# The transfer queue of a fused convolution and expert kernel: issue order by the program instead of by the scheduler

## The chip, the cores and the metric

The program runs on one core of a Trainium2 chip. The metric is the device time of one execution in microseconds. Before the change the median of three runs is 1215.89 us (1215.02 to 1219.19). The profile was taken on a fourth execution.

## The reference, cut to what matters

```python
def _attn_ref(x, weight_gen):                 # x: 8 x 3584 x 192, weight_gen: 8 x 3584 x 8 x 7
    w = np.exp(weight_gen - np.max(weight_gen, axis=-1, keepdims=True))
    w = w / (np.sum(w, axis=-1, keepdims=True) + 1e-09)
    x_pad = np.concatenate([np.zeros((B, 6, D)), x], axis=1)
    x_unf = x_pad[:, idx, :].reshape(B, S, 7, 8, 24)
    return np.einsum('bshk,bskhg->bshg', w, x_unf).reshape(B, S, D)

def _moe_ref(x, w_gate, w1, w2):              # x: 28672 x 192; 8 experts, 192 -> 1024 -> 192
    logits = x @ w_gate
    expert_idx = np.argmax(logits, axis=1)
    gate_w = softmax(logits)[arange(N), expert_idx]
    ...
    h = np.maximum(x_sorted[lo:hi] @ w1[e], 0.0)      # tokens lo:hi are those of expert e
    y_sorted[lo:hi] = h @ w2[e]
    ...
    return gate_w[:, None] * y
```

A convolution over seven tokens, whose weights differ from token to token, is followed by a layer of experts of which each token uses one.

## The kernel before, in words

**Chunks.** The 28672 tokens are cut into 28 chunks of 1024. For each chunk `load` (L304, L314) brings `w_sb` and `x_sb`; VectorE multiplies and adds the taps (L355, L379), in the first four chunks with help of TensorE (L364) and GpSimd. The sum is split into a high and a low fp16 part (`pl`), TensorE transposes it (L474) and computes the gate's logits (L486), VectorE finds expert, rank and gate factor, and `send` (GpSimd, L560) scatters the token rows into the DRAM tensor `queue`, which holds a list of rows for each expert.

**Tiles.** After each chunk `choose` picks expert tiles that can be filled from the rows written so far: 256 tokens each at first, then 384, then small ones that empty the lists, 97 in all. The number of a tile's first row is computed on VectorE and lies in a small tile `rows` (L600). `fetch(n)` brings tile n in with four steps on SyncE (SP): it loads the row number into a register (`value_load`, L732; a TENSOR_LOAD in the order), it transposes the token rows into `xt` (L744), it loads the 1796 KB of the expert's weights into `wt` (L746), and it loads the gate factors and the output rows into `meta` (L749). `xt` waits until the scatters of the chunk that the tile was chosen from have landed and until the first layer has freed the buffer three tiles before; `wt` waits for the second layer of the tile three before; `meta` waits for the output scatters of the tile four before. The program calls `fetch` of tile n+2 in the middle of tile n. For the tiles of the last chunk seven more buffers are used, so that `fetch` may run up to nine tiles ahead.

**Layers.** TensorE computes the first layer (L806) and second layer (`l2`, L712) of neighbouring tiles in alternation, ScalarE and VectorE make `hh` and `hl` (L815 to L829), and GpSimd scatters the results to the output (L560).

**Two stages.** In the first `with` block (L954 to L967) the experts' weights are loaded, normalized, split into high and low halves and stored to `wq` in DRAM (L286 to L291), beside the convolution of the first chunks. In the second (L968) the tiles run beside the convolution of the other chunks. In both, the order on each engine is made by a scheduler that simulates times, except for VectorE in the second stage: `manual_schedule` keeps that one in the program's order. SP's order is the scheduler's own, so that a step of `fetch` may stand ahead of, or behind, steps that the program wrote earlier. SP issues strictly in its order: a step that waits holds up all that stands behind it.

**Rows at the end.** `pad_queues` (called after the last chunk's `send`) writes 128 zero rows behind each expert's list by eight scatters on GpSimd, and writes the 512 dummy rows that a spare tile reads, by four transfers of SP (L635) from `padrow`, which is filled at the program's start. The scheduler placed these four in the first stage.

Of the kernel before, what the change touches and what calls it, by code (L numbers as in the profile page):

```python
# [114 lines left out]
def conv_moe_kernel(ctx: ExitStack, tc: tile.TileContext, x, wgen, w_gate, w1, w2, out):  # L115
# [135 lines left out]
    def w_norm(e):  # L251


        g = ps_y.tile([P, 2, 2 * P], F32, name="y")
        for n, f in enumerate(wsp[e]):
            v = f.bitcast(BF16)
            if n:
                v = v.rearrange("p f d -> p (f d)")
            v = v.rearrange("p (b q t) -> p b q t", q=P, t=2)
            for b in range(12):  # L260
                blk = v[:, b, :, 1]
                nc.tensor.matmul(g[:, n, 0:P], blk, blk, start=(b == 0), stop=(b == 11))
        nc.vector.tensor_reduce(stats[e], g[:, :, 0:P], axis=AX.X, op=ALU.max)

    def w_high(e, pro):
        f1, f2 = wsp[e]
        ws, h1, l1, w2v = w_views(e)
        st2 = ps_y.tile([P, 2 * 256], F32, name="y")
        nc.tensor.matmul(st2[:, 0:2], ones_f, stats[e], start=True, stop=True)
        s, i = norm_scale(st2[:, 0:2], 2, pro)  # L270
        nc.vector.tensor_tensor(ws[:, W_INV:W_INV + 2].bitcast(F32), i[:, 0:1], i[:, 1:2], op=ALU.mult)
        nc.scalar.activation(h1, f1, AF.Copy, scale=s[:, 0:1])
        nc.scalar.activation(w2v[:, :, 0, :], f2, AF.Copy, scale=s[:, 1:2])
        wsp[e].append(s)

    def w_low(e):
        f1, f2, s = wsp[e]
        ws, h1, l1, w2v = w_views(e)
        nc.vector.scalar_tensor_tensor(l1, f1, s[:, 0:1], h1, **sub)
        yield  # L280
        nc.vector.scalar_tensor_tensor(w2v[:, :, 1, :], f2, s[:, 1:2], w2v[:, :, 0, :], **sub)
        yield
        r0 = e * P
        hl = ws[:, 0:3 * F].rearrange("p (t c) -> p t c", t=2)
        tails = wq[:, O_H1:].rearrange("q (t c) -> q t c", t=2)
        nc.sync.dma_start(wq[r0:r0 + P, 0:2 * F].rearrange("p (t c) -> p t c", t=2), hl[:, :, 0:F])  # L286
        nc.sync.dma_start(wq[r0:r0 + P, O_W2:O_H1], ws[:, 3 * F:])
        for i in range(2):
            half = hl[64 * i:64 * i + 64, :, F:]
            for r in (r0, r0 + 64):  # L290
                nc.sync.dma_start(tails[r:r + 64, :, i * FH:(i + 1) * FH], half)  # L291
# [8 lines left out]
    def load(c):  # L300
        k = ch[c] = Chunk()
        k.x = cin.tile([P, J + HALO, D], F32, name="x_sb")
        k.w = cin.tile([P, J * H, KW], F32, name="w_sb")
        nc.sync.dma_start(k.w, bass.AP(wr.tensor, wr.offset + c * J * H * KW,  # L304
                                       [[NP * H * KW, P], [1, J * H * KW]]))
        if c == 0:
            nc.vector.memset(k.x[0:1, 0:HALO, :], 0.0)
            for p0, p1 in ((1, PPB), (PPB, P)):
                nc.sync.dma_start(k.x[p0:p1, 0:HALO, :],
                                  bass.AP(xr.tensor, xr.offset + (p0 * NP - HALO) * D,  # L310
                                          [[NP * D, p1 - p0], [1, HALO * D]]))
            nc.sync.dma_start(k.x[:, HALO:, :], bass.AP(xr.tensor, xr.offset, [[NP * D, P], [1, J * D]]))
        else:
            nc.sync.dma_start(k.x, bass.AP(xr.tensor, xr.offset + (c * J - HALO) * D, [[NP * D, P], [1, (J + HALO) * D]]))  # L314
# [241 lines left out]
    def scatter(dst, idx, src, grp, bound=None):  # L556
        kw = {}
        if bound is not None:
            kw = dict(bounds_check=bound, oob_is_err=False)
        st = nc.gpsimd.indirect_dma_start(out=dst, out_offset=bass.IndirectOffsetOnAxis(ap=idx, axis=0),  # L560
                                          in_=src, in_offset=None, **kw)
        tc.declare_no_dep(st.ins, group=grp, reason="every row is written once")
        if grp == "q":
            tc.declare_no_dep(st.ins, group="qr", reason="a row is read only after it was written")
        tc.add_to_no_dep_group(grp, st.ins)
        return st
# [58 lines left out]
    def pad_queues():  # L625
        padi = const.tile([P, E], I32, name="padi")
        pio = const.tile([P, 1], F32, name="pio")
        nc.gpsimd.iota(pio, pattern=[[0, 1]], base=0, channel_multiplier=1,
                       allow_small_or_imprecise_dtypes=True)
        nc.vector.tensor_scalar(padi, base[-1], pio, None, op0=ALU.add)  # L630
        for e in range(E):
            st = scatter(queue, padi[:, e:e + 1], padrow, "q")
            writers[NCH - 1].append(st.ins.name)
        for n in range(4):
            st = nc.sync.dma_start(queue[DUMMY + n * P:DUMMY + (n + 1) * P, :], padrow)  # L635
            tc.declare_no_dep(st.ins, group="q", reason="every row is written once")
            tc.declare_no_dep(st.ins, group="qr", reason="a row is read only after it was written")
            tc.add_to_no_dep_group("q", st.ins)
            writers[NCH - 1].append(st.ins.name)
# [8 lines left out]
    def finish(c):  # L648

        yield max(0.0, ch[c].sent + REST1 - clock[0])  # L650
        logits(c)
        yield from route1(c)
        ranks(c)
        yield from gate(c)
        yield from places(c)
        send(c)
        if c == NCH - 1:
            pad_queues()
        yield from choose(c)
# [209 lines left out]
    def weights(pro):  # L869

        ev = []
        for e in range(E):
            at = W_AT + W_GAP * e
            ev += [(at, e, 0), (at + W_HIGH, e, 1), (at + W_LOW, e, 2)]
        for at, e, k in sorted(ev):
            yield at
            if k == 0:
                with tc.high_priority():
                    w_norm(e)
            elif k == 1:  # L880
                with tc.high_priority():
                    w_high(e, pro)
                clock[0] += 0.6
            else:
                low_ = w_low(e)
                while True:
                    with tc.high_priority():
                        if next(low_, 0) == 0:
                            break
                    clock[0] += 1.3  # L890
                    yield at
                if e + len(stage) < E:
                    with tc.high_priority():
                        w_load(e + len(stage), pro)
# [59 lines left out]
    with tc.tile_pool(name="pro", bufs=PROB) as pro, tc.tile_pool(name="pro1", bufs=1) as pro1:  # L954
        stats = [pro1.tile([P, 2], F32, name=f"st{e}") for e in range(E)]
        stage = [pro1.tile([P, W_STAGE], F16, name=f"ws{i}") for i in range(PROB)]
        for t in stage:
            nc.gpsimd.memset(t[:, W_INV:W_INV + 16], 0.0)
        load(0)
        for e in range(len(stage)):  # L960
            w_load(e, pro)
            if e == 0:
                load(1)
        wstream[0] = weights(pro)
        clock[0] = 5.0
        while wstream[0] is not None:
            vector_step()  # L967
    with tc.manual_schedule(engines={mybir.EngineType.DVE}):  # L968
        ffw = ctx.enter_context(tc.tile_pool(name="ffw", bufs=3, reuse_waits="tile"))
        ffx = ctx.enter_context(tc.tile_pool(name="ffx", bufs=2, reuse_waits="tile"))  # L970
        ffh = ctx.enter_context(tc.tile_pool(name="ffh", bufs=2, reuse_waits="tile"))
        ffo = ctx.enter_context(tc.tile_pool(name="ffo", bufs=6, reuse_waits="tile"))
        clock[1] = clock[0] + START
        parts = experts()
        n, _ = next(parts)
        while n is not None or parts is not None:
            if n is not None:
                while len(todo) <= n and vector_step():
                    pass
                if len(todo) <= n:  # L980
                    try:
                        parts.send(False)
                    except StopIteration:
                        break
                clock[1] = max(clock[1], todo[n][4] + FETCH)
            while clock[1] > clock[0] and vector_step():
                pass
            n, _ = parts.send(True)
# [23 lines left out]
```

## Time and profile before

| | |
|---|---|
| median of three runs | 1215.89 us |
| the profiled execution | 1220.97 us |
| its span | 1219.2 us |
| TensorE busy | 1143.4 us (94%) |
| VectorE busy | 1029.0 us (84%) |
| ScalarE, GpSimd busy | 695.5 us, 649.1 us |
| mean DMA rate | 263 GB/s |

TensorE is the busiest engine; over the span it is idle for 76 us. A part of this lies ahead of the first expert tile, where VectorE is the busy one. The rest of the page has to be read by stretches, since the stage of weights (to about 130 us), the small tiles (to about 290 us), the 384-token tiles (to about 1000 us) and the emptying of the lists (from there on) have different limits.

### The profile page before, as it was taken

Reading aid. Unit: us, or ns where it says so; the run is one execution under the profiler, and the core shown is the slowest. Engines: PE = TensorE matmul, PEld = TensorE weight load, DVE = VectorE, ACT = ScalarE, POOL = GpSimd, SP = SyncE. Lnnn points to the kernel's source line nnn. Section 1 sums busy time; section 2 is a strip of 40 time slices with the busy share of each in tenths; the row PEclk is TensorE's granted clock in tenths of the full one; section 3 lists DMA queues with packets and bytes.
Section 4 is the critical chain, followed back from the end, with each engine's and each line's share of the span. In section 5 each row is a group of like instructions: output and inputs, shape, how many; then the busy total and the mean of one; then the engine's idle time right before and its main releaser. Section 6 shows DMA issues by size and latency. Waiting matters only on the chain.

```text
span 1219.2 us, 30182 instructions
## 1 busy us (share of the span) xinstructions
PE 1143.4 (94%) x11666; PEld 934.5 (77%) x11666; DVE 1029.0 (84%) x1841; ACT 695.5 (57%) x1467; POOL 649.1 (53%) x576
## 2 busy tenths in 40 slices
PE   5688299899999999999999999999999998999997
PEld 3455299887787878787878777887877886789996
DVE  7999999899999999999999999999999964232331
ACT  3547277677656666665666556666664653443442
POOL 6884737565545456655566554556555565213222
PEclk9899599999999999999999999999999998999999
DMA  9998799998798768878787877788677668999995
GB/s 267 380 331 292 248 290 298 261 287 294 249 272 238 231 213 270 268 240 226 212 270 252 249 241 231 231 263 244 226 197 236 191 198 239 344 363 328 336 312 213
DMA packets 185134, 320.94 MB, mean 263 GB/s; under 512 B 132752, under 2 KB 156434, under 8 KB 169118
## 3 DMA queue, kind: packets, MB, share of 16 engines
q1 hardware_dynamic: 162862, 273.68, 72.5%
q0 software_dynamic: 22128, 45.33, 11.2%
q8 instruction: 91, 1.49, 0.5%
q14 instruction: 53, 0.43, 0.1%
HBM read 236.17 MB, written 60.76 MB: 244 GB/s over the span
## 4 chain that ended last, share of the span: by engine, by line
PE 70%; DVE 11%; DMA 9%; issue 6%; POOL 2%; SPq 1%; ACT 1%; POOLq 0%; DVEq 0%; ACTq 0%
PE ph L806 33%; PE y L712 30%; DVE tv L355 3%; DMA wt<-wq 3%; PE ph L819 2%; PE ph L474 2%; DVE hl L829 2%; DVE acc L379 1%; DMA f<-in_moe_w_dram 1%; DMA xt<-queue 1%; DMA x_sb<-in_x_dram 1%; POOL out_dram L560 1%; PE ph L364 1%; PE pm L486 1%; DMA wq<-ws 1%
## 5 line engine op out<-in xcount | busy, mean ns | idle before, releaser
L806 PE MATMUL ph<-xt,wt 128*128 128x384 f16 (+6 forms) x3880 | 579.8, 293 | 27.5 <-DMA wt<-wq 21.1
L712 PE MATMUL y<-wt,hh 128*128 128x192 f16 (+2 forms) x3696 | 505.9, 247 | 0.0
L560 POOL DMA_INDIRECT out_dram<-o,meta x231 | 277.8, 1203 | 410.7 <-ACT o L716 366.0
L712 PE MATMUL y<-wt,hl 128*128 128x192 f16 (+2 forms) x1848 | 451.6, 247 | 0.0
L806 PEld LDWEIGHTS <-wt 128*128 128x128 f16 x3880 | 330.3, 98 | 147.1 <-DMA wt<-wq 22.2
L712 PEld LDWEIGHTS <-hh 128*128 128x128 f16 (+2 forms) x3696 | 337.2, 99 | 32.9 <-issue 0.6
L560 POOL DMA_INDIRECT queue<-pl,pos x224 | 273.3, 1220 | 112.6 <-issue 70.4
L829 DVE SCALAR_TENSOR_TENSOR hl<-ph,hh 128x384 f16<-128x384 f32 (+2 forms) x372 | 203.7, 561 | 142.5 <-ACT hh L826 136.1
L355 DVE TENSOR_TENSOR tv<-x_sb,wp 128x1536 f32<-128x1536 f32 (+1 forms) x172 | 287.3, 1675 | 4.4 <-PE ph L364 4.1
L826 ACT ACTIVATE hh<-ph 128x384 f16<-128x384 f32 (+2 forms) x372 | 184.6, 500 | 185.3 <-PE ph L806 173.7
L379 DVE TENSOR_TENSOR acc<-acc,tv 128x1536 f32<-128x1536 f32 x144 | 250.0, 1736 | 0.0
L712 PEld LDWEIGHTS <-hl 128*128 128x128 f16 (+2 forms) x1848 | 181.9, 99 | 15.2 <-issue 0.3
L815 ACT ACTIVATE hh<-ph 128x384 f16<-128x384 f32 (+1 forms) x204 | 105.0, 519 | 75.2 <-PE ph L806 71.6
L716 ACT ACTIVATE o<-y,fac 128x192 f32<-128x192 f32 (+2 forms) x231 | 91.9, 420 | 86.1 <-PE y L712 84.6
L821 ACT ACTIVATE hl<-ph 128x384 f16<-128x384 f32 (+1 forms) x204 | 104.3, 519 | 41.0 <-PE ph L819 40.5
L476 ACT ACTIVATE xg<-ph 128x1024 f16<-128x1024 f16 x84 | 82.8, 1024 | 30.7 <-PE ph L474 28.8
L364 PE MATMUL ph<-tv,identf 128*128 128x384 f32 x168 | 63.6, 518 | 11.0 <-DVE tv L355 8.5
L819 PE MATMUL ph<-hh,negi 128*128 128x384 f16 (+1 forms) x256 | 68.7, 304 | 0.0
L414 ACT ACTIVATE junk<-x_sb 128x768 bf16<-128x768 f32 (+2 forms) x56 | 48.1, 859 | 18.4 <-DVE ssq L423 8.9
L474 PE MATMUL ph<-idh,pl 128*128 128x128 f16 x672 | 53.4, 225 | 3.1 <-ACT pl L445 1.6
L364 PEld LDWEIGHTS ph<-tv,identf 128*128 128x128 f32 x168 | 31.3, 199 | 30.4 <-DVE tv L355 11.4
L449 ACT ACTIVATE pl<-acc 128x768 f16<-128x768 f32 (+1 forms) x52 | 40.0, 813 | 24.3 <-DVE acc L379 16.0
(121 smaller groups left out, 810.7 us busy)
## 6 DMA issues: line engine op xcount, KB each, us to landing
wt<-wq SPq DMA_DIRECT2D x97, 1796.0 KB
x_sb<-in_x_dram SPq DMA_DIRECT2D x27, 1344.0 KB
w_sb<-in_weight_gen_dram SPq DMA_DIRECT2D x28, 224.0 KB
wq<-ws SPq DMA_DIRECT2D x8, 772.0 KB
f<-in_moe_w_dram SPq DMA_DIRECT2D x8, 768.0 KB
f<-in_moe_w_dram SPq DMA_DIRECT2D x8, 512.0 KB
wq<-ws SPq DMA_DIRECT2D x8, 512.0 KB
wq<-ws SPq DMA_DIRECT2D x32, 128.0 KB
```

The source lines that it names most:

```text
L355: eng.tensor_tensor(out, xs, ws, op=ALU.mult)
L364: nc.tensor.matmul(ap[:, 0:m], identf, tf[:, 2 * i * D:2 * i * D + m], start=(n == 0), stop=(n == KW - 1))
L379: eng.tensor_tensor(ac, ac, t, op=ALU.add)
L560: st = nc.gpsimd.indirect_dma_start(out=dst, out_offset=bass.IndirectOffsetOnAxis(ap=idx, axis=0), in_=src, in_offset=None, **kw)
L712: nc.tensor.matmul(y, hx[:, f, sl], w2v[:, f, t, :], start=(f == 0 and k == 0), stop=(f == NF - 1 and k == 2))
L716: nc.scalar.activation(o[0:m, :], y, AF.Copy, scale=fac[0:m, s:s + 1])
L806: nc.tensor.matmul(ph[:, g], wt[:, wc + f * P:wc + (f + 1) * P], xt[:, xc, 0:T], start=(k == 0 and g == 0), stop=(k == 4), skip_group_chec ...
L815: nc.scalar.activation(hv, ph, AF.Relu, scale=SHRINK)
L819: nc.tensor.matmul(ph[:, g], negi, hv[:, g], start=False, stop=True, skip_group_check=True)
L821: nc.scalar.activation(lv, ph, AF.Relu)
L826: nc.scalar.activation(hv, ph, AF.Relu)
L829: nc.vector.scalar_tensor_tensor(lv, ph, 0.0, hv, op0=ALU.max, op1=ALU.subtract)
```

## The change: who orders SP in the second stage, and where the dummy rows are written

```diff
@@ pad_queues
             st = scatter(queue, padi[:, e:e + 1], padrow, "q")
             writers[NCH - 1].append(st.ins.name)
+
+    def pad_dummies():
         for n in range(4):
             st = nc.sync.dma_start(queue[DUMMY + n * P:DUMMY + (n + 1) * P, :], padrow)
@@ first stage
             w_load(e, pro)
             if e == 0:
                 load(1)
+        pad_dummies()
         wstream[0] = weights(pro)
@@ second stage
-    with tc.manual_schedule(engines={mybir.EngineType.DVE}):
+    with tc.manual_schedule(engines={mybir.EngineType.DVE, mybir.EngineType.SP}):
```

In the second stage SP issues in the order in which the program calls `load` and `fetch`. The four dummy writes are called in the first stage, as SP would otherwise issue them after the last chunk's `send`. Lines behind the new function move down by two or three (L744 becomes L746, L746 becomes L748, L749 becomes L751).

SP at the first tiles, before. `xt_1515`, `wt_1517` and `meta_1519` are tile 0's, `xt_1530`, `wt_1532` and `meta_1534` tile 1's; four row numbers of later tiles stand between the weights and the rows of tile 1:

```order
L744 DMA_TRANSPOSE xt_1515<-queue_84 128x3x256
L746 ISA
L746 DMA wt_1517<-wq_85 128x7184
L749 ISA
L749 DMA meta_1519<-queue_84 128x2x2
L746 ISA
L746 DMA wt_1532<-wq_85 128x7184
L732 TENSOR_LOAD rows_1484
```

After, from tile 0's weights (`wt_1521`) to tile 1's (`wt_1536`):

```order
L748 DMA wt_1521<-wq_85 128x7184
L751 ISA
L751 DMA meta_1523<-queue_84 128x2x2
L734 TENSOR_LOAD rows_1275
L734 ISA x2
L746 ISA
L746 DMA_TRANSPOSE xt_1534<-queue_84 128x3x256
L748 ISA
L748 DMA wt_1536<-wq_85 128x7184
```

Tile 1's weights stood ahead of tile 1's transpose, and now stand behind it.

SP at tiles 8 and 9 before, where `xt_2822` is of tile 9, `wt_2652` of tile 8, and `x_sb_2831` is a chunk of the convolution:

```order
L744 DMA_TRANSPOSE xt_2822<-queue_84 128x3x256
L314 DMA x_sb_2831<-in_x_dram 128x2688
L746 ISA
L746 DMA wt_2652<-wq_85 128x7184
L749 ISA
L749 DMA meta_2654<-queue_84 128x2x2
L304 DMA w_sb_3349<-in_weight_gen_dram 128x448
```

After, from behind tile 8's weights (`wt_2656` is the transfer before the first row) to the same chunk (`x_sb_2835`):

```order
L751 DMA meta_2658<-queue_84 128x2x2
L734 TENSOR_LOAD rows_2311
L734 ISA x2
L746 ISA
L746 DMA_TRANSPOSE xt_2826<-queue_84 128x3x256
L748 ISA
L748 DMA wt_2828<-wq_85 128x7184
L751 ISA
L751 DMA meta_2830<-queue_84 128x2x2
L304 DMA w_sb_2836<-in_weight_gen_dram 128x448
L314 DMA x_sb_2835<-in_x_dram 128x2688
```

The next tile's transpose and the chunk's `x_sb` stood ahead of a tile's weights; now each tile's weights follow its own transpose, and the chunk comes behind the weights of two tiles.

SP in the last chunk, before, at tile 67 (`wt_16270`): behind its weights come ten row numbers, and only then its rows, `xt_16268`:

```order
L732 TENSOR_LOAD rows_16298
L732 ISA x2
L746 ISA
L746 DMA wt_16270<-wq_85 128x7184
L732 TENSOR_LOAD rows_16375
L732 ISA x2
```

After, the same tile, with its transpose first:

```order
L734 TENSOR_LOAD rows_15919
L734 ISA x2
L746 ISA
L746 DMA_TRANSPOSE xt_16268<-queue_84 128x3x384
L748 ISA
L748 DMA wt_16270<-wq_85 128x7184
```

Tile 67's weights moved from ahead of its transpose to behind it. In both programs that transpose waits for the last of the eight scatters of `pad_queues`. Between the early tiles and the last chunk the SP order reads the same in both but for the row numbers, which come one for each tile instead of in blocks, and for `w_sb` ahead of `x_sb`. VectorE's order differs only in the first 270 or so of its rows, where the stage of weights hands over: the last expert's two low halves (L279, L281) come earlier.

## Rows read from the trace of the kernel before

**Rows 1.** The busy time of the engines over the span, and the sizes of two transfers, from the page:

```profile
PE 1143.4 (94%) x11666; PEld 934.5 (77%) x11666; DVE 1029.0 (84%) x1841; ACT 695.5 (57%) x1467; POOL 649.1 (53%) x576
wt<-wq SPq DMA_DIRECT2D x97, 1796.0 KB
x_sb<-in_x_dram SPq DMA_DIRECT2D x27, 1344.0 KB
```

**Rows 2.** Windows: length, then busy time of each engine (and instructions), the granted clock, the DMA share and GB/s, in five stretches of the run:

```profile
120.00:160.00 40.00, 17.82 (x178) 15.23 (x176) 36.27 (x69) 13.83 (x27) 28.12 (x22) 0.63 0.80 253
200.00:240.00 40.00, 36.52 (x402) 33.83 (x400) 36.10 (x56) 26.25 (x54) 24.22 (x19) 0.96 0.93 269
...
320.00:630.00 310.00, 309.97 (x3090) 247.18 (x3088) 303.33 (x536) 194.89 (x423) 175.26 (x146) 1.00 0.82 244
630.00:730.00 100.00, 98.04 (x957) 77.79 (x955) 99.97 (x180) 59.55 (x133) 57.97 (x45) 1.00 0.76 241
...
1160.00:1200.00 40.00, 40.00 (x666) 39.96 (x664) 12.89 (x20) 17.69 (x40) 9.74 (x11) 1.00 0.98 346
```

**Rows 3.** What TensorE waited for from 133 to 320 us and, below the line of dots, from 990 us to the end (us in total, times, longest):

```profile
PE ph L806 <- DMA wt<-wq: 18.6, 4, 12.4
...
PE ph L806 <- DMA xt<-queue: 4.4, 1, 4.4
```

**Rows 4.** The timeline of SP's queue at the start of the second stage (start, duration, what):

```profile
134.86 1.34 SPq L744 DMA_TRANSPOSE xt<-queue  x1
136.74 0.37 SPq L746 DMA_DIRECT2D wt<-wq  x1
...
137.97 0.33 SPq L746 DMA_DIRECT2D wt<-wq  x1
146.88 1.39 SPq L744 DMA_TRANSPOSE xt<-queue  x1
```

**Rows 5.** The timeline of TensorE there; the last bracket is the idle time before and what ended it. Between the two rows of the second layer (L712) stand ten more of its matmuls:

```profile
145.79 5.66 PE L806 MATMUL ph<-xt,wt 128*128 128x256 f16 x32 [12.45 <-DMA wt<-wq]
151.51 1.04 PE L806 MATMUL ph<-xt,wt 128*128 128x256 f16 x8
...
152.60 0.33 PE L712 MATMUL y<-wt,hh 128*128 128x192 f16 x2
...
154.06 0.33 PE L712 MATMUL y<-wt,hh 128*128 128x192 f16 x2
154.23 2.35 PE L806 MATMUL ph<-xt,wt 128*128 128x256 f16 x20
```

**Rows 6.** The timeline of GpSimd: the last of the eight scatters of chunk 1 and of chunk 2.

```profile
123.76 3.71 POOL L560 DMA_INDIRECT queue<-pl,pos  x1 [0.30 <-issue]
139.91 1.37 POOL L560 DMA_INDIRECT queue<-pl,pos  x1 [0.30 <-issue]
```

**Rows 7.** From the chain of work, the pieces between 200 and 285 us in which a tile's weights were under way, and a piece of the second layer (start, duration, what):

```profile
215.49 12.44 DMA wt<-wq
249.45 10.88 DMA wt<-wq
270.19 1.99 PE y L712 x24
272.30 9.45 DMA wt<-wq
```

**Rows 8.** SP's queue around the first two of these:

```profile
212.59 0.38 SPq L749 DMA_DIRECT2D meta<-queue  x1
213.36 1.21 SPq L744 DMA_TRANSPOSE xt<-queue  x1
214.67 0.53 SPq L314 DMA_DIRECT2D x_sb<-in_x_dram  x1
215.49 0.33 SPq L746 DMA_DIRECT2D wt<-wq  x1
...
243.70 0.34 SPq L314 DMA_DIRECT2D x_sb<-in_x_dram  x1
```

**Rows 9.** What TensorE waited for from 630 to 730 us:

```profile
PE ph L806 <- DVE hl L829: 1.9, 2, 1.7
```

**Rows 10.** SP's queue in the last chunk, and, below the dots, the end of the pad scatters in the chain of work:

```profile
1006.80 0.34 SPq L746 DMA_DIRECT2D wt<-wq  x1
1020.14 1.33 SPq L744 DMA_TRANSPOSE xt<-queue  x1
...
1017.73 2.39 DMA queue<-padrow,padi
```

**Rows 11.** TensorE's timeline around tile 67's first matmul:

```profile
1018.96 1.79 PE L806 MATMUL ph<-xt,wt 128*128 128x384 f16 x10
1025.13 1.76 PE L806 MATMUL ph<-xt,wt 128*128 128x384 f16 x5 [4.38 <-DMA xt<-queue]
```

**Rows 12.** What SP waited for most from 1095 to 1130 us (us in total, times, longest):

```profile
SPq L746 <- PE y L712: 10.5, 4, 3.5
```

**Rows 13.** TensorE's timeline at the end:

```profile
1202.29 1.17 PE L806 MATMUL ph<-xt,wt 128*128 128x32 f16 x40 [1.41 <-DMA wt<-wq]
1206.66 1.16 PE L806 MATMUL ph<-xt,wt 128*128 128x16 f16 x40 [1.12 <-DMA wt<-wq]
```

**Rows 14.** The dummy rows' transfers in SP's timeline:

```profile
8.32 2.57 SPq L635 DMA_DIRECT2D queue<-padrow  x4
```

## The prediction

> **What bounds the kernel now.** I read the busy times first, then windows, then what ended the waits of the busiest engine, and last the queue that feeds it. TensorE is busy for 94% of the span [rows 1], but the share hides where the rest is. From 320 to 630 us it is full; from 630 to 730 us VectorE is full and TensorE loses 2 us [rows 2], waiting for the low halves of `h` [rows 9]. So in these 410 us an order of transfers has next to nothing to win, and the change leaves SP's order there as it was. TensorE's gaps that a transfer ends are few: 18.6 us for weights from 133 to 320 us, 4.4 for a transpose behind 990 us [rows 3] and 2.5 for the last two weights [rows 13], 25.5 us in all. They are what the change can win; what it can lose is that a step that waits on SP holds up what is queued behind it.
>
> The time is made against the profiled execution, 1220.97 us, which is 5.1 us above the median of the three runs; I work out a difference and take it off the median.
>
> **The dummy rows.** The four transfers of L635 were issued at 8.32 us already, 2.57 us of SP's queue [rows 14]. After the change they stand in the same stage, some places later. TensorE's first expert tile is over 130 us away: nothing.
>
> **The first two tiles.** Before, tile 0's transpose went out at 134.86 us [rows 4], although the last scatter of its chunk ended at 127.47 (123.76 + 3.71) [rows 6]; between the two SP stood before four row numbers of the next chunk. That block is gone. With a landing of 2.39 us, as a later scatter of the same kind took [rows 10], the transpose can go at 127.5 to 129.9; I take 129. Its weights follow 1.9 us behind (136.74 less 134.86), at 131. Before, they came 9.05 us later (136.74 to 145.79 [rows 4, 5]) with a second set of 1796 KB beside them; alone, at 346 GB/s [rows 2], 1.84 MB take 5.3 us. So tile 0 starts at 136 to 140, I take 138, against 145.79: some 8 us. They are not won, for tile 1's weights, which before went out at 137.97, right behind tile 0's, now stand behind tile 1's transpose, which waits for the scatters of chunk 2. The last of these ended at 141.28 [rows 6]; with a landing of 2.39 that is 143.7, and as it was, 146.88 [rows 4]. Weights 1.9 us behind, landing after 5.3 to 9.05: 150.9 to 157.8, I take 154.3, the middle. What TensorE has until then is tile 0: first layer 6.7 us (5.66 + 1.04, mostly at a low clock [rows 5]) and 48 matmuls of the second layer at 0.083 us (1.99 for 24 [rows 7]), 4 us, twice that at the lower of the two clock levels. From 138 it is through at 149 to 153 and waits again. Before, tile 1's first layer began at 154.23 [rows 5] with 14 of these 48 matmuls done, 2.8 us of work outstanding, which is like beginning at 157.0 with tile 0 finished. The gain is therefore 157.0 less 154.3, **2.7 us**; from the ends of the landing it is +6.1 to -0.8. A second spell at the low clock, if TensorE idles again before tile 1, costs up to 2.2 us more: the 32 matmuls took 5.66 us, and 32 at the 0.109 us of the next tile (20 in 2.35, the first end being late) would take 3.5.
>
> **The early tiles, 200 to 285 us.** Three sets of weights are on the chain for 12.44, 10.88 and 9.45 us [rows 7], more than the 5.3 of a transfer alone. In front of the first, SP issued the next tile's transpose and `x_sb`, 214.67 against 215.49; in front of the second, at 243.70, again `x_sb` [rows 8]. 1344 KB [rows 1] at 346 GB/s are 4.0 us of the DMA engines that the weights had to share. After the change that `x_sb` stands behind the weights of two tiles. TensorE's loss there is 6.2 us (18.6 less the 12.45 of the first tile [rows 3, 5]), and the clock, 0.96 from 200 to 240 us [rows 2], lost 1.6 us more (4% of 40). Ends: 0, since `meta` held SP until 212.59 and still stands ahead of the next weights [rows 8], and 7.8 if all goes. I take **4 us**, one `x_sb`: the 3.5 us that TensorE was idle from 200 to 240 us (40 less 36.52 [rows 2]) are about what this transfer takes.
>
> The Trainium skill, "DMA: Bandwidth & Descriptors", section "Queues, rings and completion order", says that each DMA engine consumes a queue's descriptors in ring order. By that rule the whole 4.0 us of `x_sb` come off the weights behind it; if the two shared the engines evenly, about half would. The row that bears on it, 12.44 us against 5.3, leaves room for either, and the sum would be 4 or 2 here.
>
> **What the full VectorE takes back.** From 630 to 730 us VectorE sets the pace: a start that is 6.7 us earlier passes through only if VectorE is earlier too. It has idle time ahead, 6.7 us from 320 to 630 and 3.9 from 200 to 240 [rows 2], part of which ends with TensorE's results, so most of it should pass. I take three quarters: 6.7 becomes **5.0**. If nothing passes, 0.
>
> **The last chunk.** Tile 67's transpose waits for the last pad scatter, which landed at 1020.12 (1017.73 + 2.39 [rows 10]), in both orders. Before, its weights went out ahead, at 1006.80; now they follow, not before 1021.7 (1020.14 + 1.33, and the gap), and take 5.3 to 9 us: 1027 to 1030.7. TensorE was idle from 1020.75 (1018.96 + 1.79) to 1025.13 [rows 11]. In the new order the second layer of tile 66, 48 matmuls or 3.95 us, comes ahead of tile 67's first layer and needs nothing of tile 67: it fills most of that wait, and TensorE then waits from 1024.7 for the weights. Before, the same 3.95 us were still to be done at 1025.13, which is like beginning tile 67 at 1029.1. Against 1027 to 1030.7 that is a gain of 2.1 or a loss of 1.6 us. The other cost is 1.84 MB moved from an idle stretch into one in which DMA runs full to the end: 5.3 us if nothing absorbs it. But from 1095 to 1130 us SP waits 10.5 us for buffers that the second layer frees [rows 12]: the ring of buffers is full then, and a delay of 5.3 us is gone. I take **0**, with the ends -6.9 (1.6 and 5.3) and +2.1.
>
> **The end.** TensorE waits 1.41 and 1.12 us for the last two sets of weights [rows 13], with the DMA share at 0.98 before that [rows 2]. In the new order each set follows its own transpose rather than two later ones, and the second layer of tile 95 comes ahead of the wait for the last weights, where it fills it. I take **2 us** of the 2.5, with ends 0 and 4.5 (2.5, and 2 for matmuls at the lower clock that follow the last gap).
>
> **The sum.** 5.0 + 0 + 2 = 7.0 us. From 1220.97 that is 1214.0; from the median, 1215.89 less 7.0, **1209 us**.
>
> **The rivals.**
>
> *A waiting transpose holds up the weights behind it* (slower). This is one mechanism at two places, tile 1 and tile 67. It costs if tile 1's weights land at the late end, 157.8 us (-0.8, and -2.2 for the clock), and if tile 67's land after 1029.1 (-1.6) and the 5.3 us of DMA are not absorbed by the full ring. Then 0.8 + 2.2 + 1.6 + 5.3 = 9.9 are lost, and the early tiles and the end give 3/4 of 4 and 2 back: 1215.9 + 4.9, about 1221. For it speaks that SP stood from 1006.80 to 1020.14 [rows 10] with nothing issued; against it, the waits for full buffers [rows 12]. It decides once tile 67's weights come later than 1029.1 and SP finds no full ring behind. The Trainium skill says in the same page, section "Anatomy of one DMA", that a DMA's semaphore wait is spent on the issuing sequencer before it is dispatched. The 13 us of [rows 10] agree.
>
> *The pace of VectorE eats it* (no change). What is won before 630 us is lost in the full stretch, and the end alone stays: 1215.9 less 2, about 1214. For it: 99.97 of 100 us [rows 2]; against it: TensorE lost only 1.9 us to `hl` there [rows 9], so the two are near balance.
>
> *The early stalls are not of the order* (the change doesn't do there what its order suggests). The 12.44 us come from `meta`, which waits for output scatters, and these are as late as before. Then the 4 of the early tiles are gone and 3/4 of 2.7 plus 2 remain: 1212, at the edge of no change.
>
> *All of it goes*: 6.1 at the start, 7.8 at the early tiles, nothing lost to VectorE, 2 at the end: 15.9, about 1200.
>
> **How the numbers follow.** Chances: the forecast with its own range of 1204 to 1212 us, 0.48; the waiting transpose, 0.17; VectorE's pace, 0.15; the early stalls stay, 0.14; all of it, 0.06. A measurement of this kernel can tell 0.3%, 3.6 us, from no change, so faster means below 1212.2 and slower above 1219.5. Faster: nearly all of the forecast (0.45), half of the stalls' case (0.07), all of it (0.06): 0.58. Slower: most of the first rival, 0.16. The rest, 0.26, is no change. The range goes from 1202 to 1219 us: below it lies most of the 0.06, above it most of the 0.17.
>
> **What would show it.** Right: tile 0's first matmul at 136 to 140 us and tile 1's at 151 to 157 with a second gap of 2 to 6 us; TensorE's waits for weights from 200 to 285 us under 3 us; the wait at tile 67 between 2 and 6 us with full TensorE from there to 1160; the last two gaps under 1 us together. Wrong: a gap at tile 1 of 8 us or more, a lower clock behind it, idle time of TensorE on `hl` from 630 to 730 us above 5 us (VectorE's pace), or waits for weights spread from 1030 to 1160 us (the DMA delay not absorbed). New waits of VectorE for `x_sb` or `w_sb`, of which the trace of before shows none worth naming, would make the forecast wrong from a side that the sum leaves out.

## The result, and the profile after

The changed kernel takes **1226.23 us** (median of five runs, 1224.72 to 1227.66), the kernel before 1215.89 on the same chip (1214.6 to 1219.87): a ratio of 1.0076, with a 95% interval of 1.0053 to 1.0098. It is slower, by about 10 us; the prediction was 1209, range 1202 to 1219. The profiled executions are 1227.66 and 1220.97 us, their spans 1226.0 and 1219.2. So the two traces differ by 6.8 us of the 10.3: the trace of before comes from an execution 5.1 us above its median, the one after from one 1.4 above, and what the other 3.6 us consist of no trace here shows.

Three groups of the runs below stood on chips on which the kernel before takes 1320, 1322 and 1347 us. In the traces from there the engines stand idle in the middle of the run without a wait that the profile shows ("issue"), so the whole time tells little, and single stages are read.

To place the loss I counted the first layer's matmuls in program order, and took the start of the first one of each tile (us from the span's start):

| | tile 0 | tile 1 | tile 13 | 16 to 41 | 43 to 66 | 66 to 67 | 67 to 75 | 75 to 92 | 92 to 96 |
|---|---|---|---|---|---|---|---|---|---|
| before | 145.79 | 154.23 | 281.80 | 341.94 | 315.99 | 15.75 | 91.11 | 74.80 | 15.62 |
| after | 140.28 | 152.90 | 281.76 | 343.25 | 318.20 | 21.98 | 86.92 | 74.80 | 19.68 |

The lead of 5.5 us at tile 0 is gone at tile 13. Then 3.7 us are lost up to tile 66 (1.3 and 2.2 in the two stretches of the table). At tile 67 6.2 are lost, of which 4.2 come back by tile 75, because the second layer of tile 66 has been done meanwhile. At the end 4.1 are lost; 3.0 come back behind the last first layer, where only one second layer is left instead of two. That sums to the 6.8.

The stretch of the first tiles, after: first SP's queue (start, duration, what), then TensorE (the bracket is the idle time before). They answer to [rows 4, 5].

```profile
129.10 1.33 SPq L746 DMA_TRANSPOSE xt<-queue  x1
130.97 0.39 SPq L748 DMA_DIRECT2D wt<-wq  x1
...
141.50 1.29 SPq L746 DMA_TRANSPOSE xt<-queue  x1
143.05 0.37 SPq L748 DMA_DIRECT2D wt<-wq  x1
```

```profile
140.28 6.09 PE L808 MATMUL ph<-xt,wt 128*128 128x256 f16 x32 [9.84 <-DMA wt<-wq]
152.90 6.38 PE L808 MATMUL ph<-xt,wt 128*128 128x256 f16 x30 [3.10 <-DMA wt<-wq]
```

Tile 1's weights go out behind tile 1's rows, 5 us later than before, and are used 9.8 us after. TensorE idles a second time, and tile 1 runs at the lower clock too (granted: 0.53 from 152 to 159.3 us, before 1.00): 30 matmuls in 6.38 us, where before 20 took 2.35.

What TensorE waits for, after: 133 to 320 us, 320 to 990, and 990 to the end, with dots between (us in total, times, longest), for [rows 3, 9]:

```profile
PE ph L808 <- DMA wt<-wq: 18.5, 6, 9.8
...
PE ph L808 <- DVE hl L831: 1.6, 3, 0.9
PE ph L808 <- DMA wt<-wq: 1.0, 1, 1.0
PE ph L808 <- ACT hl L823: 0.9, 2, 0.5
PE y L714 <- ACT o L718: 0.8, 2, 0.4
...
PE ph L808 <- DMA wt<-wq: 9.6, 2, 6.6
```

In the middle there are new waits for ScalarE, and ScalarE has a new one of its own. From ScalarE's waits of 320 to 990 us, a row that has no counterpart before, and the queue and TensorE around it:

```profile
ACT junk L414 <- DMA x_sb<-in_x_dram: 6.4, 3, 3.2
```

```profile
843.33 0.35 SPq L748 DMA_DIRECT2D wt<-wq  x1
844.03 0.38 SPq L751 DMA_DIRECT2D meta<-queue  x1
844.52 0.45 SPq L304 DMA_DIRECT2D w_sb<-in_weight_gen_dram  x1
845.05 0.64 SPq L314 DMA_DIRECT2D x_sb<-in_x_dram  x1
```

```profile
875.76 0.97 PE L808 MATMUL ph<-xt,wt 128*128 128x384 f16 x5 [0.43 <-ACT hl L823]
882.53 0.97 PE L808 MATMUL ph<-xt,wt 128*128 128x384 f16 x5 [0.92 <-DVE hl L831]
```

ScalarE waits for a chunk's `x_sb` (L414 squares it), which on SP stood behind weights that waited for their buffer; the tiles' own work stands behind L414 on ScalarE. Before, the same chunk's `x_sb` went out 15 us earlier, ahead of the same weights:

```profile
829.68 0.42 SPq L314 DMA_DIRECT2D x_sb<-in_x_dram  x1
...
841.88 0.34 SPq L746 DMA_DIRECT2D wt<-wq  x1
```

This holds for the whole stretch: each of the 16 `x_sb` loads that before went out from 311 to 866 us now stands behind one more set of weights. That SP's order between the early tiles and the last chunk reads the same in both, as the section on the change has it, is therefore wrong.

The last chunk, SP's queue and TensorE, for [rows 10, 11], and then the window around the late start, after and (below the dots) before:

```profile
1001.38 0.36 SPq L748 DMA_DIRECT2D wt<-wq  x1
1001.96 0.38 SPq L751 DMA_DIRECT2D meta<-queue  x1
1023.82 1.32 SPq L746 DMA_TRANSPOSE xt<-queue  x1
1025.44 0.35 SPq L748 DMA_DIRECT2D wt<-wq  x1
```

```profile
1035.03 5.64 PE L808 MATMUL ph<-xt,wt 128*128 128x384 f16 x20 [6.65 <-DMA wt<-wq]
1209.84 1.22 PE L808 MATMUL ph<-xt,wt 128*128 128x32 f16 x40 [2.97 <-DMA wt<-wq]
```

```profile
1032.00:1040.00 8.00, 4.97 (x17) 2.43 (x18) 0.00 (x0) 1.09 (x3) 0.00 (x0) 0.57 1.06 297
...
1024.00:1032.00 8.00, 6.87 (x36) 4.60 (x37) 0.00 (x0) 1.43 (x4) 1.97 (x2) 0.59 1.09 323
```

SP issues nothing for 22 us; tile 67's weights, which before went out 13 us ahead of its rows, go out behind them and are used 9.6 us later, and the matmuls that follow run at a granted clock of 0.57. That clock is no loss against before, where the gap at tile 67 had it too (0.59).

### The profile page after: what moved, and what is told of

It is laid out like the page before. It is cut to its first block, busy times and chain, and to the rows that moved or that the text cites. A ratio compares the mean times of both kernels' runs of the same rounds, so it can differ in the third digit from the quotient of the medians.

```text
span 1226.0 us, 30163 instructions
## 1 busy us (share of the span) xinstructions
PE 1147.8 (94%) x11666; PEld 932.4 (76%) x11666; DVE 1028.3 (84%) x1841; ACT 697.5 (57%) x1467; POOL 654.8 (53%) x576
## 4 chain that ended last, share of the span: by engine, by line
PE 58%; DVE 16%; DMA 13%; issue 7%; POOL 2%; SPq 2%; ACT 1%; POOLq 0%; DVEq 0%; ACTq 0%
PE ph L808 28%; PE y L714 25%; DMA wt<-wq 7%; DVE tv L355 4%; DMA x_sb<-in_x_dram 3%; DVE acc L379 3%; DVE hl L831 2%; PE ph L474 2%; DMA queue<-pl,pos 2%; PE ph L821 2%; DMA f<-in_moe_w_dram 2%; POOL out_dram L560 1%; PE pm L486 1%; DVE acc L355 1%; SPq L746 1%
## 5 line engine op out<-in xcount | busy, mean ns | idle before, releaser
L560 POOL DMA_INDIRECT out_dram<-o,meta x231 | 284.8, 1233 | 414.6 <-ACT o L718 371.7
L831 DVE SCALAR_TENSOR_TENSOR hl<-ph,hh 128x384 f16<-128x384 f32 (+2 forms) x372 | 204.5, 563 | 151.9 <-ACT hh L828 146.2
L560 POOL DMA_INDIRECT queue<-pl,pos x224 | 269.0, 1201 | 111.5 <-issue 62.9
L823 ACT ACTIVATE hl<-ph 128x384 f16<-128x384 f32 (+1 forms) x204 | 103.5, 519 | 34.5 <-PE ph L821 33.7
L414 ACT ACTIVATE junk<-x_sb 128x768 bf16<-128x768 f32 (+2 forms) x56 | 48.1, 860 | 26.9 <-DMA x_sb<-in_x_dram 16.8
```

The lines of the kernel that those rows point to most:

```text
L823: nc.scalar.activation(lv, ph, AF.Relu)
L831: nc.vector.scalar_tensor_tensor(lv, ph, 0.0, hv, op0=ALU.max, op1=ALU.subtract)
```

## The experiments

The theories. **A**: the blocked queue; a step that waits on SP now holds up weights (tile 67) and `x_sb` (tiles 16 to 66). **B**: the dummy rows' place in the first stage. **C**: TensorE's own order, which the scheduler made anew. After the third group a fourth was added, **D**: the stream of the last 28 sets of weights takes the same time in any order, so that the end follows its start.

**The kernel before again, and the dummy rows alone.** The second is the changed kernel with `engines={mybir.EngineType.DVE}` put back.

> The kernel before, unchanged, for a second profile. The theory of the blocked queue (A: on SP a step that waits now holds up weights and x_sb behind it, at tile 67, in the 384-token stretch and at the end) and its rivals (B: the dummy rows' new place in the first stage costs the time; C: the order in which TensorE alternates layers costs it, not SP) all expect a ratio of 1.000 +- 0.002. The profiled execution should come nearer to the median of 1216 us than the first one of 1220.97; then tile 0 to 15 are where the two profiles of the same kernel part.

> The dummy rows are written in the first stage, SP stays with the scheduler. A and C: within 2 us of the kernel before, about 1216. B: most of the 10 us, 1222 or more.

Measured, on a chip with 1319.69 us for the kernel before: ratios of 1.0014 (0.9984 to 1.0044) and 1.0005 (0.9971 to 1.0038). B falls, and later runs agree: g1 and h3 below keep the dummy rows in the first stage and are not slower. The execution did not come out at 1216; the waits of TensorE in e1_before_again show why:

```profile
PE y L712 <- issue: 18.2, 27, 1.7
PE ph L806 <- DMA wt<-wq: 17.1, 4, 12.2
PE ph L806 <- issue: 12.4, 17, 2.3
PE pm L486 <- issue: 12.4, 15, 2.2
PE ph L474 <- issue: 11.4, 22, 1.2
```

The four "issue" rows, waits for nothing that the profile shows, are absent from the trace of before. What makes a chip do this was not tried.

**Late weights first.**

```diff
+        first = sent[0] == NCH - 1
+        if not first:
             rows_of(nc.sync.dma_start_transpose(xt[:, :, 0:T], ...))
         nc.sync.dma_start(wt, wq[ds(e * P, P), :])
+        if first:
+            rows_of(nc.sync.dma_start_transpose(xt[:, :, 0:T], ...))
```

> The changed kernel, but a fetch that is called after the last chunk's scatters issues its weights ahead of its transpose. A: tile 67's weights go out at about 1005 us instead of 1025, the wait for weights of 6.65 us at tile 67 becomes one for rows of about 4, one set of weights less is moved in the stretch where DMA is full, and the time is 1226 - 4 to 6 = 1220 to 1222. C: TensorE's order stays, so the gain is under 1 us. B: no gain.

**A split fetch**: row number and `xt` in the tile's second group, `wt` and `meta` in its last one.

```diff
+        yield None                       # between xt and wt
...
+                    if todo[m][3] < NCH - 1 and m <= n + 2 and t < groups - 1:
+                        half.append((m, fetch2(m)))
+                        next(half[-1][1])
+                        done_.append(m)
...
+                while t == groups - 1 and half:
+                    m, rest_ = half.pop(0)
+                    loaded[m] = next(rest_)
```

> The changed kernel, but for tiles before the last chunk fetch is cut in two: row number and transpose where they were, weights and meta in the tile's last group, where the second layer that frees the buffer has been issued, so that x_sb isn't queued behind weights that wait. A: ScalarE's waits for x_sb from 320 to 1000 us (6.4 us) go, tiles 20 and 56 lose their +1.3 and +2.2 us against before, and the time is 1226 - 3.5 = 1222 to 1223, with tile 67 and the end as in the changed kernel. C and B: no change, 1226.

Measured on the same chip: 0.9959 (0.9922 to 0.9997) and 1.0155 (1.0112 to 1.0197). The changed kernel was not among them, so the first says nothing yet. The second is slower through a mistake of the edit: a further fetch could begin while one was half done, so that transfers of later tiles came ahead of tile 68's weights. It is the blocked queue once more, at a higher price:

```profile
1172.46 5.63 PE L814 MATMUL ph<-xt,wt 128*128 128x384 f16 x20 [19.45 <-DMA wt<-wq]
```

**The changed kernel beside them, with the split mended** (`not half and` ahead of the condition of the other fetch) **and the pads apart**:

```diff
             st = scatter(queue, padi[:, e:e + 1], padrow, "q")
+            tc.add_to_no_dep_group(f"s{NCH - 1}", st.ins)
```

With this line tile 67's transpose, whose rows earlier chunks wrote, doesn't wait for the eight pad scatters, which write behind those rows.

> The changed kernel, unchanged, beside the next three on their chip. Expected 1.0076 times the kernel before (interval of the first measurement 1.0053 to 1.0098), with the late tiles in the same places: +1.3 us at tile 20, +2.2 at tile 56, a wait for weights of 6 to 7 us at tile 67. [...]

> The kernel of e4_late_weights_first again, now beside the changed kernel. A (the blocked queue): 4 to 6 us below the changed kernel, tile 67's wait for weights gone. C (TensorE's own order): within 1 us of the changed kernel.

> As e5_split_fetch, but no further fetch may begin while one is half done; before, tile 68's transpose, which waits for the last chunk's scatters, stood ahead of tile 67's weights, and tile 68 began 36 us behind tile 67. A: that gap is gone, ScalarE's waits for x_sb from 320 to 1000 us are under 1 us, and the time is 3 to 4 us below the changed kernel. If x_sb's place is not what costs tiles 20 and 56 their time, it is within 1 us of the changed kernel.

> The changed kernel, but the eight pad scatters count as written with the last chunk, so that tile 67's transpose, whose rows were written by earlier chunks, doesn't wait for them. A: tile 67's rows and weights go out right behind tile 66's, at about 1005 us instead of 1024, TensorE waits for neither at tile 67, and the time is 6 to 8 us below the changed kernel: 1218 to 1220. C: less than 1 us.

Measured (1322.21 us for the kernel before): 0.9938 (0.9907 to 0.9969), 0.9973 (0.9935 to 1.0012), 0.9993 (0.9958 to 1.0028), 0.9930 (0.9888 to 0.9972). The changed kernel is *faster* than before here, and beside it (median 1312.03 us) none of the three cures is (1319.49, 1320.06, 1314.38): the gain that A expected of them did not come on this chip. The stages say more:

| 1320 us chips | tile 13 | 13 to 66 | 66 to 67 | 92 to 96 | 66 to 96 |
|---|---|---|---|---|---|
| e1 (order of before) | 298.92 | 825.9 | 11.20 | 15.99 | 190.5 |
| e3_after_again | 286.11 | 823.5 | 15.16 | 18.75 | 193.4 |
| late weights first, twice | 285.27 / 285.19 | 823.2 / 829.7 | 12.77 / 12.42 | 20.04 / 22.24 | 196.1 / 198.0 |
| split, mended | 279.61 | 830.3 | 15.30 | 18.39 | 193.2 |
| pads apart | 289.18 | 822.7 | 12.42 | 16.47 | 192.2 |

From tile 66 on the changed kernel is some 3 us slower than e1 here. What it wins lies ahead of that, where two executions of "late weights first" differ by 6.5 us in "13 to 66"; whether it comes from the order was not settled. At tile 67 these traces do not tell A from C. The changed kernel's 15.2 us hold no wait, as its row there shows, without a bracket:

```profile
1124.73 3.41 PE L808 MATMUL ph<-xt,wt 128*128 128x384 f16 x20
```

They are longer because TensorE's order has 48 matmuls of tile 66's second layer (4 us) ahead of tile 67 here, and behind its start in e1 and with the pads apart. By tile 75 the changed kernel is 99.9 us behind tile 66's start, e1 99.7, the pads apart and late weights first 100.9 to 101.3. The transpose had gone out 6 us ahead of tile 66's start on this chip, against 11 us behind it in the changed kernel's first trace. Weights ahead of rows in all late tiles cost at the end, 20 to 22 us instead of 18.8.

**Three of them on another chip**; f7 joins the split and the pads apart.

> The kernel of e4_late_weights_first, on another chip if one is given on which the kernel before takes 1216 us; there the changed kernel took 1226.2. A (the blocked queue): tile 67's weights go out some 20 us earlier, its wait for weights of 6.65 us becomes a wait for rows of 3 to 4, and the time is 1220 to 1222, 1.004 times the kernel before. C (TensorE's own order): 1226, 1.008.

> The kernel of e5_split_mended, likewise. A: ScalarE's waits for x_sb (6.4 us from 320 to 1000 us) are under 1 us, tiles 20 and 56 stand where they stood before, and the time is 1222 to 1223, 1.005 to 1.006 times the kernel before. If x_sb's place is not the cause of tiles 20 and 56: 1226, 1.008.

> The kernel of e6_pads_apart, likewise. A: TensorE waits for nothing at tile 67, and the time is 1218 to 1220, 1.002 to 1.004 times the kernel before. C: 1226, 1.008.

> Both changes of f5 and f6. A: the two gains add up, 1214 to 1217, 0.999 to 1.001 times the kernel before, since what is left against it is the end, where the last weights come late. C: 1226, 1.008.

Measured (1346.96 us for the kernel before): 0.9988 (0.9954 to 1.0021), 0.9975 (0.9937 to 1.0013), 0.9892 (0.9818 to 0.9965), 0.9959 (0.9927 to 0.9992). Tile 66 to 67: 11.20, 16.15, 11.20, 11.20 us, of which the split's, the one that keeps the pads as they were, again holds the 48 matmuls; 92 to 96: 22.25, 20.05, 16.70, 17.63. The reading at the end repeats; the rest is inconclusive.

**Pads apart and split, on a chip with 1217 us.**

> The kernel of f6_pads_apart. [...] On a chip with 1216 us for the kernel before: A expects 1218 to 1221 (the changed kernel 1226), C 1226.

> The kernel of f5_split. On a chip with 1216 us for the kernel before, A expects 1222 to 1223 and tiles 20 and 56 where the kernel before has them; 1226 if x_sb's place isn't what costs them their time. [...]

Measured (1217.25 us for the kernel before): pads apart **1217.32**, 1.0016 (0.9996 to 1.0036); split 1227.97, 1.0102 (1.0076 to 1.0128). One line takes the ratio from 1.0076 to 1.0016, some 7 us of 1217 (9 by the medians, which are from two chips; the two kernels stood side by side only on the 1322 us chip). Tile 67's rows and weights in SP's queue of g1_pads_apart:

```profile
997.60 3.70 SPq L747 DMA_TRANSPOSE xt<-queue  x1
1005.69 0.35 SPq L749 DMA_DIRECT2D wt<-wq  x1
```

The weights go out 20 us earlier than in the changed kernel's trace (15 counted from tile 66's start), and TensorE has no wait at tile 67. From tile 66's start to the end the changed kernel takes 212.9 us and the split, which keeps the wait, 213.0; pads apart takes 207.0. So the trace gives 5.9 us to the wait: 8.5 by tile 75, and 2.6 given back at the end. Another 4.8 us between these two traces lie ahead of tile 66 (4.0 of them at tile 13), where SP and TensorE have the same order in both. They are not the line's: the kernels with this order scatter by as much at tile 13 (277.7 to 281.8). The 5.9 us, and the 6.65 us of idle TensorE that weights ended, are what speaks for A at tile 67. The split removes what it was made for, ScalarE's wait for `x_sb`, and stays slow (A had 1222 to 1223): the wait at tile 67 remains (6.4 us), and late weights cost as much elsewhere, for TensorE's only wait of any size from 320 to 990 us is a new one at tile 42.

```profile
675.40 0.50 PE L814 MATMUL ph<-xt,wt 128*128 128x384 f16 x1 [4.08 <-DMA wt<-wq]
```

**The start of the last stream.** h1 is the kernel before with the pads apart. h2 is the changed kernel with the pads apart, eight `meta` buffers, and the weights of the last chunk's first four tiles ahead of their rows; h3 has the pads apart and the buffers alone; h4 is h2 with fetch called from the tile's middle group on.

```diff
-        meta = px.tile(..., bufs=AHEAD + 1 if ring else 4)
+        meta = px.tile(..., bufs=AHEAD + 1 if ring else 8)
...
+        if late and n == lates[1]:
+            for m in range(n, n + RING):           # RING is 4
+                r, e = first(m)                    # row number and expert
+                early[m] = r, weights_of(e, lates[0])
...
-                if t >= 1 and len(done_) < len(todo):
+                if t >= 1 and len(done_) < len(todo) and (todo[len(done_)][3] == NCH - 1 or t >= groups // 2):
```

> The kernel before, with the pad scatters counted as the last chunk's. A in its present form (D: the 28 sets of weights from tile 69 on move in 158 to 160 us whatever the order, so that the end follows the time at which tile 69's weights go out): tile 67's wait of 4.4 us goes, but tile 69's weights go out at about 1030 as before, so the last tile's are no earlier, and the time is within 2 us of the kernel before, while the waits for weights at the end grow by about 4. Against D: 4 to 6 us faster.

> The changed kernel with the pad scatters apart, eight meta buffers instead of four, and the weights of the last chunk's first four tiles issued ahead of their rows. D: tile 69's weights go out at about 1019 instead of 1039, the waits for the last weights are gone, and TensorE is full from 1000 us on: 8 to 10 us below the kernel before, about 1207 on a chip with 1216; 4 or 5 us of it are lost if the early stretch and x_sb's waits cost what they cost in the profile of the changed kernel. Against D: not below g1_pads_apart, 1.000 to 1.002 times the kernel before.

> g1_pads_apart with eight meta buffers: tile 68's meta held SP there from 1018.5 to 1028.8 us for the output scatters of an earlier tile. D: tile 69's weights go out some 5 us earlier than in g1 (1031.8), limited by the scatters of the last chunk, the last tile's follow, and the time is 2 to 5 us below g1, 0.997 to 1.000 times the kernel before. Against D: as g1.

> h2_ring_weights_first, with fetch called from the middle group of a tile on (before the last chunk) instead of the second group, so that weights wait less on SP and x_sb less behind them. If x_sb's place is worth the 3.5 us of tiles 20 and 56: ScalarE's waits for x_sb are halved at least, and it is 1 to 3 us below h2. If moving weights later costs as much, as at tile 42 of g2_split (4.1 us): the same as h2 or slower.

Measured (1217.90 us for the kernel before): h1 1215.45, 0.9982 (0.9970 to 0.9994); h2 1215.98, 0.9983 (0.9967 to 0.9999); h3 **1214.16**, 0.9973 (0.9959 to 0.9988); h4 1216.38, 1.0000 (0.9982 to 1.0018). The stages of this group and the one before it:

| 1217 us chips | tile 13 | 16 to 41 | 43 to 66 | 66 to 67 | 67 to 75 | 92 to 96 |
|---|---|---|---|---|---|---|
| h1 (order of before) | 281.88 | 342.04 | 315.99 | 11.20 | 88.48 | 19.14 |
| g1 pads apart | 277.73 | 342.63 | 317.75 | 11.20 | 89.22 | 20.88 |
| h2 | 281.24 | 342.89 | 317.56 | 11.20 | 89.27 | 17.94 |
| h3 | 277.90 | 342.82 | 318.18 | 11.20 | 89.02 | 17.39 |
| g2 split | 273.69 | 342.28 | 315.26 | 21.70 | 86.03 | 20.98 |
| h4 | 275.89 | 342.28 | 315.99 | 11.20 | 89.44 | 19.04 |

h3 came out as D expected: tile 69's weights went out 5.5 us earlier than in g1, the last set 4.7 earlier, and the ratio is 0.9973. D falls with h2 all the same. In its queue of SP the first four sets went out together, 8 us ahead of the first of them in g1 (1031.78), and still the 81st and the last, below the dots, are not earlier than in g1, where they are at 1092.35 and 1190.59:

```profile
1023.76 4.41 SPq L752 DMA_DIRECT2D wt<-wq  x4
1028.59 18.38 SPq L764 DMA_TRANSPOSE xt<-queue  x1
...
1092.18 0.35 SPq L752 DMA_DIRECT2D wt<-wq  x1
...
1190.16 0.36 SPq L752 DMA_DIRECT2D wt<-wq  x1
```

Counted from tile 66's start, which h2 has 3.5 us later than g1, its 70th set goes out 11.5 us ahead of g1's. The transpose behind the four sets then holds SP for 18 us; the 74th set is 1.2 us ahead, the 81st 3.7, and at the 84th nothing is left (103.5 us in both). There the ring is full: in all eight traces from such chips the 84th set goes out 34.6 us ahead of its tile's first matmul (after: 1125.00 and 1159.62; before: 1119.31 and 1153.91). So the ring of buffers does make up for a late start, as the prediction said. What remains is the stretch after it: from the 84th set's issue to tile 96's first matmul 87.4 us before and 90.9 in h1, 91.4 after, and 89.1 to 92.6 in g1, h2, h3 and h4. The two orders overlap there; what makes the end of the changed kernel 4 us longer than in the trace of before, with DMA full in both, is open, and no run isolates it. And `x_sb`: in "43 to 66" the kernels whose ScalarE waits for `x_sb` (after, g1, h2, h3) need 317.6 to 318.2 us, those without that wait (before, h1, g2, h4) 315.3 to 316.0. The 2 us hold in all eight traces, and most of them lie at tile 56, two tiles behind the wait (16.39 us against 14.71), besides some 0.6 to 1.3 in "16 to 41". Fetching later, as h4 does, wins these 2 us and does not lower the whole time: its tiles 13 to 16 take 43.9 us, in h2 40.1.

## Why the prediction was wrong

Of the 7.0 us that the sum won, the two traces give 0 up to tile 13, where it had 6.7; 3.7 lost from there to tile 66, where it had 1.7 for VectorE; 2.0 lost at the last chunk by tile 75, where it had 0; and 1.1 lost at the end, where it had 2 won. That is 6.8 us lost.

**The first two tiles: right in mechanism, and the cost that was left out of the sum came.** Tile 0 was forecast at 136 to 140 us and began at 140.28, tile 1 at 151 to 157 and began at 152.90, with a gap of 3.10 us. The second spell at the low clock, priced at up to 2.2 us and not put into the sum, took 6.38 us for 30 matmuls, 2.9 more than at the rate of the trace of before (20 in 2.35). The gain was smaller, too: the sum had tile 0 finished before tile 1 began, but only 20 of its 48 second-layer matmuls were done (before, 14), which leaves 2.3 us of work. By the sum's own count tile 1 began like one at 155.2 with tile 0 finished, against 157.0: 1.8 us won, 2.9 lost.

**The early tiles: the step failed.** I expected 4 us from `x_sb` standing behind the weights instead of ahead of them. The waits for weights behind tile 1 were 5.6 us (18.5 less 9.84 and 3.10) against 6.2. An `x_sb` that is taken from ahead of one tile's weights stands ahead of a later tile's, and DMA moves as much: 283 and 298 GB/s from 200 to 240 and 240 to 285 us, before 269 and 287. At tile 13 the four kernels with this order on 1217 us chips stand at 277.7 to 281.8, the order of before at 281.8 and 281.9: a gain of 0 to 4 us for both steps together, where 6.7 was the term. The rival of the early stalls, at 0.14, had this outcome; whether they come from `meta`, as it says, was not tried. The Trainium skill ("DMA: Bandwidth & Descriptors", "Queues, rings and completion order"), by which descriptors are consumed in ring order, was weighed here for 4 us; the waits got shorter by 0.6 us in all, so the case neither shows nor refutes it.

**The middle: a step that failed, a cost without a term.** The prediction named new waits for `x_sb` as what would make it wrong from outside the sum. They came, through ScalarE instead of VectorE, and are worth 2 to 3.5 us between tiles 16 and 66 (0.6 to 1.3, and some 2). The step that failed is the reading that the change leaves SP's order there as it was: each chunk's `x_sb` had moved behind one more set of weights, and inherits their wait for a buffer (829.68 before, 845.05 after, and 3.16 us of ScalarE's time at tile 54). I had taken an unchanged order as a reason for no cost, and put no term.

**VectorE's pace** took nothing: TensorE's waits for `hl` are 1.6 us, before 1.9.

**The last chunk: mis-sized.** I took 0, with the end of the range at -6.9. Tile 67's weights were put at 1021.7 with a landing at 1027 to 1030.7. They went out at 1025.44, since all was 3.7 us late by then, and were used at 1035.03, 9.6 us later where 5.3 to 9 was taken. Against before it is 6.2 us at the tile, 2.0 by tile 75, as the second layer of tile 66 was indeed done meanwhile. Against the same kernel without the wait it is more: 5.9 us from tile 66 to the end, and the ratio goes from 1.0076 to 1.0016. But the order of before has a wait there too. How much of the difference between the two kernels the wait makes is therefore open: by the traces the order of before pays nearly as much for it (209.9 us from tile 66 to the end, 204.5 in h1), by the ratios less (0.2% against 0.6%). The rival of the waiting transpose, at 0.17, had the mechanism and the place, and came too low at 1221. Its condition, that the full ring absorbs nothing, was wrong: the 84th set goes out 34.6 us ahead of its tile in all eight traces, however late the stream began.

**The end: the wrong sign.** Instead of 2 us won, 1.1 are lost (4.1 less the 3.0 of the second layer that moved ahead). One gap of 2.97 us stands where two of 1.41 and 1.12 stood: the sets from the 84th to the last took 74.0 us to go out, before 68.8. Why is open.

**The dummy rows** cost nothing that shows, as forecast (1.0005, interval 0.9971 to 1.0038).

## What to carry to other kernels

On a queue that issues strictly in order, list for each step that may wait what is queued behind it, and price the gap and the clock after it; here one needless wait, that of a transpose for scatters of other rows, cost 5.9 us from tile 66 to the end in the program's order and 5.3 in the scheduler's (by the ratios 0.6% and 0.2% of the whole time). Look first whether the wait is needed at all: eight pad scatters declared apart and four more small buffers give a version that is 0.27% faster than the kernel before and, by the two ratios, 1% faster than the changed one. Compare two orders of a queue step by step over their whole length: here one load for each chunk had moved behind one more set of weights, and it inherits the wait of the step ahead of it.

## What was not expected of the hardware

The same program took 1216, 1320 and 1347 us on different chips, with "issue" waits on TensorE's matmuls that add up to 54 us in the four rows of e1_before_again and to none in the trace of before. Of two kernels 0.8% apart, the slower on one chip was 0.6% faster on another.
